# A gated recurrence with a channel MLP behind it: last chunk's second product and store in two parts, new orders and engines for most steps

## Chip, core and metric

The kernel runs on one core of one Trainium2 chip. The core has five engines that run their own instruction lists side by side: PE (TensorE: matmuls and weight loads), DVE (VectorE), ACT (ScalarE), POOL (GpSimd) and SP (SyncE, which here only issues DMAs). POOL issues DMAs too, on a queue of its own. The metric is the time of one execution on the device in microseconds (us).

## The reference

```
attention part, for each batch (4) and head (8), D = 48, t = 0 .. 767:
    mag = sqrt(a_re^2 + a_im^2);  a = (a_re, a_im) * min(mag, 0.999) / (mag + 1e-6)
    S = a * S (complex, a over the rows of S) + (k_t outer v_t, real)
    y_t = q_t @ S_re
x = y, heads side by side: 4 x 768 rows of 384
MLP part, for each row of x:
    xn = (x - mean) / sqrt(var + 1e-6) * g_ln
    out = x + max(xn @ w_ch1, 0) @ w_ch2         # w_ch1 384 x 1536, w_ch2 1536 x 384
```

## The kernel before

The 4 x 768 rows are cut into 24 chunks of 128 rows, six for each batch. Consecutive chunks form nine groups (0 holds chunk 0, 1 holds chunks 1 and 2, 2 holds 3 to 5, and so on by threes; 8 holds 21 to 23), and the groups form six phases.

**Gate steps of a group.** From the loaded a: `rec` (ln and exp of a_re on ACT), `r` = ai times that (one step for each chunk, on DVE or POOL), `r2` = its square, `l1p` (ACT), `lm` (DVE, L425), `cap` (DVE, L432: min with a constant, in place). PE sums the logarithms along the rows with a triangular matrix (`l_ps`, L438), and ACT makes `ep` and `en` of it (`epn`, L443). Another table of ACT is then loaded (L370) and the arctan of r taken (L493). `carry` steps add whole chunks, PE sums the angle (`th_ps`, L530 to L534), ACT takes the sine, DVE shifts by a quarter turn (`w`, L547), ACT takes the cosine. `qk` (L582) multiplies q by ep and k by en, `stk` (L588) multiplies both by sine and by cosine.

**Attention of a chunk.** stk is transposed to `qkt`: for chunks 0 to 11 by PE (`heads`, L615) and a copy by ACT or DVE, for chunks 12 to 23 by a transposing DMA that SP issues (L628). PE makes the scores (`a_ps`, L640), DVE masks them (`at`, L644), PE makes `y_ps` (L666, L668), and the state goes on to the next chunk by `t_ps` (PE) and `s` (DVE, L716).

**MLP of a chunk.** `x` is copied from y_ps, its moments are taken (`bn` on DVE, L737, or sums on ACT, L732), POOL makes `rs` for three chunks (L742, L743), x is transposed to `xt` (PE and a copy, or a DMA by SP, L756), `up` is the first product (`h_ps`, L778, 36 matmuls of 128 columns in parts of 24 and 12), `relu` (ACT L784 or DVE L786) makes `ht`, `down` is the second product (`o_ps`, L799, 12 matmuls of 384 columns), `residual` (DVE, L803) scales and adds x, `store` (SP, L807) writes 192 KB.

**Weights.** w_ch1 comes in three loads of 512 columns (`w1r`, POOL's queue, 384 KB each in SBUF) and is folded with g_ln: `centring` makes a matrix from g_ln (`gln`, one small load), PE multiplies it with w1r (`means`, `w_ps`, L318), DVE makes `w1c` (L322, three steps for each load). w_ch2 comes as three loads (`w2b`). The inputs of batch 0 are loaded chunk by chunk (a by SP, q and k by POOL), those of later batches six chunks at a time by POOL.

**What sets the order.** Every step is recorded in a plan with its engine, a cost, what it needs and what it makes. The kernel then issues all steps in one list, `HOW["order"]`, which holds their numbers; each engine runs its own steps in that order and waits where one is not ready. Where a step can run on several engines, a string in `HOW` has one letter for each step (A, V, P for ACT, DVE, POOL). `HOW["fill"]` names steps of PE ahead of which identity matmuls run that fill the step's own PSUM tile and are overwritten (L169 for bf16 tiles, L173 for others: 512 columns each in a wide tile). Some of DVE's and POOL's steps, cap among them, carry a flag `port` in the plan.

Of the kernel before, what the change touches and what calls it, by code (L numbers as in the profile page):

```python
# [10 lines left out]
FP32 = mybir.dt.float32  # L11
# [3 lines left out]
ALU = mybir.AluOpType  # L15
# [5 lines left out]

LOADS = {"a": ("ar", "ai"), "s": ("q", "k", "v"), "qk": ("q", "k"), "v": ("v",)}
HOW = {'loads': [('a', 0, 1, 'Y'), ('a', 1, 2, 'Y'), ('a', 2, 3, 'Y'), ('a', 3, 4, 'Y'), ('a', 4, 5, 'Y'), ('a', 5, 6, 'Y'),
           ('g', 0, 0, 'P'), ('w1', 0, 0, 'P'), ('w1', 1, 0, 'P'), ('w1', 2, 0, 'P'), ('qk', 0, 1, 'P'),
           ('qk', 1, 2, 'P'), ('qk', 2, 3, 'P'), ('qk', 3, 4, 'P'), ('qk', 4, 5, 'P'), ('qk', 5, 6, 'P'),
# [5 lines left out]
 'ar2': 'PPPPPPPPPPPPPPPPPPPPPPPP',  # L33
 'ai2': 'PPPPPPPPPPPPPPPPPPPPPPPP',
 'm2': 'PPPPPPPPPPPPPPPPPPPPPPPP',
 'r2': 'PVAVVAAAAVVVVVVVVVVVVVVV',
 'r': 'VVVVVVVVVPVVVPPPPPPPPPPP',
 'carry': 'VVVVPVVVVVPVVVVVPVVPVVVV',
 'st': 'AVVVVVAA',
 'x': 'AAAVAAAVAAVAAAAVAAAAAAAA',  # L40
 'edge': 'YYYYYYYYYYYYYYYYYYYYYYYY',
 'cos': 'VVVVVVVVVVVVVVVVVVVVVVVV',
 'qt': 'AAAAAVVVAVVVAAAAAAAAAAAA',
 'kt': 'AVVVAAVAVVVVVVVVVVVVVVVV',
 'relu': 'AAAVVVAAAAAVAVAAAVAAVAAAAAAAAVVVAAAAAAAAAAVAAAAA',
 'qk': 'PPVVVVPVPPVPVVVVVVVVVVVVVVVVVVVVVVVVVVVVVVVVVVVV',
 'stk': 'PVVVVVVVVVVVVVVVVVVVVVVVVVVVVVVVVVVVVVVVVVVVVVVV',
 'at': 'VVVVVVVVVVVVVVVVVVVVVVVV',
 'xc': 'AVAAAVAAVAVVVVVVVVVVVVVV',
 'xt': 'PPPPPPPPPPPPDDDDDDDDDDDD',  # L50
 'qkt': 'PPPPPPPPPPPPDDDDDDDDDDDD',
 'order': [5, 20, 38, 199, 8, 4, 12, 36, 40, 14, 16, 22, 18, 200, 201, 24, 202, 9, 203, 11, 28, 212, 44, 213, 46, 204,
           215, 48, 214, 42, 216, 186, 217, 1, 205, 191, 0, 206, 50, 218, 207, 54, 219, 208, 6, 193, 220, 209, 210,
           52, 221, 32, 2, 222, 34, 75, 7, 10, 225, 232, 231, 235, 226, 227, 236, 192, 238, 228, 26, 243, 229, 233,
           187, 239, 230, 240, 30, 68, 234, 241, 188, 470, 223, 246, 472, 190, 194, 66, 247, 242, 195, 237, 189, 248,
           197, 478, 60, 479, 471, 249, 62, 250, 473, 251, 56, 245, 252, 3, 244, 79, 253, 198, 64, 493, 516, 196, 494,
           495, 254, 81, 518, 517, 255, 496, 256, 480, 257, 474, 481, 258, 475, 259, 501, 503, 261, 519, 58, 497, 260,
           502, 476, 504, 264, 262, 520, 498, 265, 278, 499, 524, 500, 266, 521, 267, 268, 477, 505, 77, 483, 269,
           506, 484, 272, 88, 482, 522, 525, 487, 523, 271, 270, 528, 507, 485, 273, 529, 275, 274, 279, 526, 510,
           276, 486, 508, 95, 280, 277, 530, 282, 281, 532, 488, 511, 540, 283, 538, 541, 489, 531, 102, 284, 533,  # L60
           509, 563, 285, 539, 527, 512, 286, 287, 564, 288, 542, 109, 289, 513, 584, 490, 546, 561, 290, 534, 562,
           585, 547, 291, 543, 292, 548, 294, 582, 535, 295, 293, 544, 549, 545, 297, 569, 565, 296, 583, 551, 300,
           298, 310, 566, 586, 491, 514, 587, 301, 567, 568, 116, 302, 306, 570, 303, 307, 550, 552, 588, 308, 304,
           572, 311, 555, 123, 589, 305, 553, 573, 556, 312, 309, 592, 610, 574, 554, 313, 314, 611, 571, 602, 604,
           593, 315, 612, 603, 625, 605, 646, 316, 626, 606, 627, 607, 647, 317, 557, 628, 130, 319, 318, 575, 320,
           608, 629, 613, 576, 321, 630, 594, 577, 322, 137, 609, 648, 595, 615, 596, 323, 616, 327, 597, 324, 329,
           578, 590, 328, 325, 649, 591, 326, 614, 330, 633, 332, 343, 536, 558, 650, 617, 651, 333, 579, 631, 618,
           634, 334, 335, 580, 559, 632, 652, 342, 635, 336, 338, 654, 337, 339, 636, 619, 653, 340, 637, 655, 172,
           638, 341, 620, 344, 346, 598, 144, 345, 347, 658, 348, 670, 659, 599, 668, 671, 691, 600, 364, 350, 676,
           669, 693, 677, 714, 639, 692, 351, 640, 715, 365, 712, 349, 672, 694, 641, 660, 368, 673, 352, 366, 713,  # L70
           695, 353, 674, 696, 367, 621, 675, 158, 369, 354, 678, 370, 355, 681, 679, 356, 656, 642, 661, 371, 657,
           358, 357, 716, 372, 151, 682, 373, 717, 662, 374, 697, 663, 375, 376, 698, 699, 378, 359, 622, 664, 361,
           701, 377, 392, 360, 643, 381, 680, 644, 702, 362, 683, 703, 665, 623, 382, 404, 666, 704, 379, 684, 383,
           700, 391, 395, 384, 705, 718, 396, 385, 387, 719, 386, 388, 722, 685, 389, 706, 393, 390, 397, 707, 394,
           400, 398, 401, 723, 732, 740, 399, 686, 738, 726, 739, 402, 687, 741, 403, 753, 405, 406, 408, 724, 772,
           407, 409, 798, 759, 734, 410, 799, 760, 708, 735, 792, 727, 412, 725, 720, 736, 755, 721, 737, 728, 426,
           756, 743, 411, 427, 709, 813, 688, 774, 413, 757, 775, 778, 430, 758, 414, 762, 779, 776, 428, 729, 794,
           777, 747, 832, 415, 795, 429, 745, 165, 431, 416, 782, 800, 746, 796, 801, 815, 689, 797, 432, 764, 710,
           179, 816, 803, 819, 417, 765, 817, 433, 418, 748, 834, 419, 766, 835, 786, 420, 434, 421, 818, 784, 423,
           821, 822, 422, 761, 767, 435, 730, 785, 749, 780, 424, 454, 437, 802, 436, 438, 742, 768, 440, 439, 781,  # L80
           467, 443, 787, 805, 466, 444, 750, 824, 806, 457, 445, 769, 446, 825, 820, 770, 458, 449, 447, 453, 836,
           826, 450, 448, 837, 788, 840, 451, 455, 452, 751, 462, 456, 459, 463, 807, 789, 460, 850, 464, 844, 808,
           858, 845, 461, 842, 790, 827, 871, 838, 465, 856, 809, 468, 839, 843, 857, 890, 859, 469, 852, 828, 853,
           441, 854, 910, 829, 877, 855, 873, 846, 874, 861, 810, 878, 892, 931, 875, 893, 916, 896, 876, 897, 880,
           894, 912, 895, 918, 913, 811, 860, 863, 900, 898, 917, 919, 914, 830, 864, 847, 950, 865, 933, 915, 882,
           934, 920, 848, 879, 921, 902, 866, 899, 867, 903, 904, 935, 905, 884, 883, 937, 952, 885, 938, 923, 936,
           953, 940, 868, 925, 924, 954, 869, 926, 886, 955, 939, 958, 906, 887, 888, 944, 907, 960, 908, 945, 962,
           942, 927, 943, 956, 963, 957, 946, 961, 964, 947, 928, 929, 948, 965, 966],
 'fill': {227: 2.67, 256: 0.26, 470: 0.81, 493: 2.49}}


class Plan:
# [32 lines left out]
def kernel(  # L125
# [14 lines left out]
    C = 128  # L140
    NCH = S // C
    NG = B * NCH
    DM = H * D
    DF = moe_w_ch1.shape[1]
    NJ = DF // C
# [11 lines left out]
    moe = pool("moe", 2)  # L157
    V, A, P, T, Y = nc.vector, nc.scalar, nc.gpsimd, nc.tensor, nc.sync
    BY = {"V": V, "A": A, "P": P, "Y": Y}
    ENG = {V: "V", A: "A", P: "P", T: "T", Y: "Y"}  # L160

    fill = [0.0]
# [27 lines left out]
    def op(eng, us, needs, makes, fn, *a, **kw):  # L190
        if eng is T:
            kw["lag"] = 0.14
        return plan.add(ENG[eng], us, (fn, a), needs, makes, **kw)
# [31 lines left out]

    def load(eng, g0, g1, names, after=()):
        b, c0, c1 = g0 // NCH, g0 % NCH, g0 % NCH + g1 - g0
        us = 0.5 if eng is Y else 0.66 + 0.26 * (c1 - c0)
        for n in names:
            issue(eng, us, [("in_" + n, b)], load_fn, (eng, b, n, c0, c1), c1 - c0,  # L230
                  1.0, [("got_" + n, b, c) for c in range(c0, c1)])

    def over_sp(us, moves, lag, needs, makes, fn, *a, **kw):
        key = ("sp",) + makes[0]
        used = list(kw.pop("uses", ()))
        plan.add("Y", us, (fn, a), needs, makes + [key], uses=used, **kw)
        plan.add("Q", moves, None, [key], makes, uses=list(needs) + used, lag=lag, ring="Y")
# [58 lines left out]
    w2b = consts.tile([C, NJ, DM], BF16, name="w2b")  # L296
# [306 lines left out]
    stats = {}  # L603
# [123 lines left out]
    def feed(g):  # L727
# [65 lines left out]
            opt("relu", 2 * g + (j0 > 0), dict(A=0.17 + 0.107 * m, V=0.16 + 0.132 * m), [("h_ps", g, j0)], [("ht", g)],  # L793
                relu, j0, j1)

        def down():
            ps = ch["o_ps"] = narrow("o_ps", [C, DM])
            for i in range(NJ):
                T.matmul(ps, lhsT=ch["ht"][:, i], rhs=w2b[:, i], start=(i == 0), stop=(i == NJ - 1))  # L799

        def residual():
            ch["o"] = moe.tile([C, DM], FP32, tag="o", name="o", bufs=3)
            V.scalar_tensor_tensor(out=ch["o"], in0=ch["o_ps"], scalar=stats[u, "rs"][:, ds(j, 1)],  # L803
                                   in1=ch["x"], op0=ALU.mult, op1=ALU.add)

        def store():
            Y.dma_start(out=out[g // NCH, ts(g % NCH, C)], in_=ch["o"])  # L807

        op(T, 1.97, [("ht", g)] + [("W2", n) for n in range(3)], [("o_ps", g)], down, takes="nar")
        op(V, 0.61, [("o_ps", g), ("rs", u), ("x", g)], [("o", g)], residual)  # L810
        over_sp(0.35, 0.9, 1.5, [("o", g)], [("out", g)], store)


    w1v = moe_w_ch1.rearrange("(i p) j -> p i j", p=C)
# [6 lines left out]
    for what, g0, g1, eng in HOW["loads"]:  # L821
        if what not in LOADS:
            load_w(P, *weights[what, g0])
        else:
            load({"Y": Y, "P": P}[eng], g0, g1, LOADS[what])
    op(V, 0.5, [("gln",), ("c_ones",)], [("centre",)], centring, port=True)
    for n in range(DF // 512):
        fold(n)
# [43 lines left out]
```

## Time and profile before

| | us |
|---|---|
| median of 3 runs (lowest, highest) | 208.03 (207.81, 209.25) |
| profiled execution, its own time | 209.94 |
| span of that execution | 208.1 |
| PE busy | 172.7 (83%) |
| DVE busy | 158.3 (76%) |
| ACT busy | 150.6 (72%) |
| POOL busy | 95.0 (46%) |
| 36 x 24 matmuls h_ps, L778 | 54.4 |
| 12 x 24 matmuls o_ps, L799 | 50.2 |
| residual, L803, 24 steps of 0.611 | 14.4 |

The profile shows one execution, with times from the start of its span. Busy time leaves out waits and the issuing of DMAs. PE's matmuls are pipelined, so a matmul's own duration is longer than the distance to the next one: 48 matmuls of h_ps follow each other within 2.68 us. A row names line, engine, operation and tiles; "idle before <-" says what ended the engine's wait. SPq and POOLq are the queues that issue DMAs.

### The profile page before, as it was taken

How to read it: one execution, taken by the hardware profiler on the slowest of the kernel's cores; microseconds unless marked ns; L12 is line 12 of the kernel's file. 1: busy time of each engine (PE TensorE's matmuls, PEld its weight loads, DVE VectorE, ACT ScalarE, POOL GpSimd, SP SyncE). 2: the span in 40 equal slices, each digit the busy share in tenths (PEclk: the TensorE clock that was granted, in tenths of full speed). 3: DMA queues.
4: the chain of work that ended last, by engine and by line, in shares of the span. 5: the costliest groups of instructions: out<-in, count | busy, mean ns of one | idle time of the engine just before them, and what ended most of it. 6: DMA issues, size and time to landing. Idle time of an engine off the chain costs nothing.

```text
span 208.1 us, 5401 instructions
## 1 busy us (share of the span) xinstructions
PE 172.7 (83%) x2287; PEld 134.8 (65%) x2287; DVE 158.3 (76%) x258; ACT 150.6 (72%) x211; POOL 95.0 (46%) x87
## 2 busy tenths in 40 slices
PE   0008969789879899999989989997999896999992
PEld 0003449669657788777956767696777665988861
DVE  0156599999879999799999999899699974606202
ACT  2247697998959999989997969896996614456150
POOL 5099698265092916699879300992210400020020
PEclk9999975999999999999999999999999998899999
DMA  6999999999999999997998919799992999723303
GB/s 101 206 180 154 200 87 148 225 115 219 166 78 143 137 238 197 123 184 71 160 161 175 265 54 269 157 215 176 161 88 71 164 206 201 194 78 55 99 3 113
DMA packets 124932, 31.44 MB, mean 151 GB/s; under 512 B 117420, under 2 KB 123276, under 8 KB 124908
## 3 DMA queue, kind: packets, MB, share of 16 engines
q0 software_dynamic: 78720, 16.52, 90.4%
q1 hardware_dynamic: 46188, 14.57, 32.0%
q8 instruction: 18, 0.29, 0.6%
q14 instruction: 6, 0.05, 0.1%
HBM read 28.31 MB, written 4.72 MB: 159 GB/s over the span
## 4 chain that ended last, share of the span: by engine, by line
PE 37%; DVE 17%; issue 13%; POOL 11%; DMA 10%; ACT 6%; SPq 4%; POOLq 0%; ACTq 0%; DVEq 0%
PE o_ps L799 12%; PE h_ps L778 11%; DMA ar<-in_a_re_dram 4%; POOL qk L213 4%; DVE stk L588 3%; DMA xt<-x 3%; DMA qkt<-stk 3%; DVE w L547 3%; PE qk_ps L169 2%; DVE at L644 2%; POOL ai L213 2%; SPq L628 2%; PE a_ps L640 2%; PE qk_ps L615 2%; PE th_ps L173 2%
## 5 line engine op out<-in xcount | busy, mean ns | idle before, releaser
L778 PE MATMUL h_ps<-xt,w1c 128*128 128x128 bf16 x864 | 54.4, 221 | 1.6 <-DMA xt<-x 1.3
L778 PEld LDWEIGHTS <-w1c 128*128 128x128 bf16 x864 | 50.5, 99 | 3.1 <-DMA xt<-x 1.5
L799 PE MATMUL o_ps<-w2b,ht 128*128 128x384 bf16 x288 | 50.2, 326 | 0.2 <-ACT ht L784 0.2
L784 ACT ACTIVATE ht<-h_ps 128x1024 bf16<-128x1024 f32 (+1 forms) x37 | 29.7, 821 | 14.9 <-PE h_ps L778 14.9
L799 PEld LDWEIGHTS <-ht 128*128 128x128 bf16 x288 | 27.4, 98 | 17.0 <-ACT ht L784 0.3
L644 DVE TENSOR_TENSOR at<-a_ps,mask 128x1024 bf16<-128x1024 f32 x24 | 29.2, 1220 | 6.4 <-PE a_ps L640 5.9
L742 POOL TENSOR_SCALAR rs<-mv 128x3 f32<-128x3 f32 x8 | 3.6, 450 | 52.0 <-ACT junk L732 33.4
L803 DVE SCALAR_TENSOR_TENSOR o<-o_ps,rs,x 128x384 f32<-128x384 f32 x24 | 14.4, 611 | 14.3 <-PE o_ps L799 10.3
L443 ACT ACTIVATE epn<-l_ps 128x384 bf16<-128x384 f32 (+1 forms) x32 | 18.7, 652 | 5.3 <-PE l_ps L438 5.3
L391 POOL TENSOR_TENSOR r<-ai,m 128x384 bf16<-128x384 f32 x12 | 11.7, 999 | 16.5 <-ACT m L412 16.5
L640 PE MATMUL a_ps<-qkt 128*128 128x128 bf16 x192 | 15.1, 223 | 2.5 <-DMA qkt<-stk 2.2
L318 PE MATMUL w_ps<-w1r,centre 128*128 128x512 bf16 x9 | 3.6, 527 | 16.2 <-DVE centre L308 15.4
L615 PE MATMUL qk_ps<-ident,stk 128*128 128x128 bf16 x192 | 13.2, 220 | 3.8 <-DVE stk L588 2.2
L370 ACT ACT_TABLE_LOAD x12 | 15.4, 1283 | 0.9 <-PEq L856 0.7
L409 ACT ACTIVATE rec<-ar 128x1152 f32<-128x1152 f32 (+2 forms) x9 | 9.5, 1055 | 8.8 <-DMA ar<-in_a_re_dram 8.7
L716 DVE TENSOR_TENSOR s<-t_ps,dec 128x384 bf16<-128x384 f32 x20 | 11.0, 551 | 6.2 <-PE t_ps L711 5.9
L391 DVE TENSOR_TENSOR r<-ai,m 128x384 bf16<-128x384 f32 x12 | 6.3, 562 | 11.4 <-DMA ai<-in_a_im_dram 9.0
L640 PEld LDWEIGHTS <-qkt 128*128 128x128 bf16 x192 | 11.7, 99 | 4.0 <-DMA qkt<-stk 2.7
L615 PEld LDWEIGHTS <-stk 128*128 128x128 bf16 x192 | 11.3, 98 | 4.6 <-DVE stk L588 1.7
L666 PE MATMUL y_ps<-v,at 128*128 128x48 bf16 x192 | 12.4, 184 | 2.2 <-DVE at L644 2.2
L582 POOL TENSOR_TENSOR epn<-qk,epn 128x1152 bf16<-128x1152 bf16 (+1 forms) x6 | 11.2, 1879 | 4.2 <-ACT epn L443 4.2
L666 PEld LDWEIGHTS <-at 128*128 128x128 bf16 x192 | 10.8, 96 | 3.5 <-DVE at L644 2.7
(102 smaller groups left out, 371.4 us busy)
## 6 DMA issues: line engine op xcount, KB each, us to landing
out_dram<-o SPq DMA_DIRECT2D x24, 192.0 KB, 3.9
ar<-in_a_re_dram POOLq DMA_DIRECT2D x3, 1152.0 KB, 10.5
ai<-in_a_im_dram POOLq DMA_DIRECT2D x3, 1152.0 KB, 11.5
v<-in_v_dram POOLq DMA_DIRECT2D x4, 576.0 KB, 10.7
qk<-in_q_dram POOLq DMA_DIRECT2D x3, 576.0 KB, 12.6
qk<-in_k_dram POOLq DMA_DIRECT2D x3, 576.0 KB, 9.5
ar<-in_a_re_dram SPq DMA_DIRECT2D x6, 192.0 KB, 5.5
w1r<-in_moe_w_ch_dram POOLq DMA_DIRECT2D x3, 384.0 KB, 6.7
```

Source lines behind the costliest of these rows:

```text
L213: eng.dma_start(out=inp[n, b].rearrange("p h c d -> p (h c) d"), in_=view.rearrange("p h c d -> p (h c) d"))
L370: op(A, 1.28, old, [key], lambda: A.preload_act_table_set(TABLES[which]))
L391: times = lambda eng, out, x, y: eng.tensor_tensor(out=out, in0=x, in1=y, op=ALU.mult)
L443: A.activation(out=o, in_=banks(G["l_ps", j], m), func=AF.Exp, scale=(1.0, -1.0)[s])
L615: T.transpose(ps[:, h], G["stk"][:, int(which == "ks"), j, ts(h, C)], K["ident"])
L640: T.matmul(ch["a"][:, h], lhsT=ch["kt"][:, h], rhs=ch["qt"][:, h], start=True, stop=True)
L644: V.tensor_tensor(out=ch["at"], in0=ch["a"], in1=K["mask"].unsqueeze(1).to_broadcast([C, H, C]), op=ALU.mult)
L666: T.matmul(hd(ps)[:, h], lhsT=ch["at"][:, h], rhs=vt[:, h, c], start=True, stop=sp is None)
L778: T.matmul(ps[:, jj], lhsT=w1c[:, i, ts(j0 + jj, C)], rhs=ch["xt"][:, i], start=(i == 0), stop=(i == ND - 1))
L784: A.activation(out=o, in_=i, func=AF.Relu)
L799: T.matmul(ps, lhsT=ch["ht"][:, i], rhs=w2b[:, i], start=(i == 0), stop=(i == NJ - 1))
L803: V.scalar_tensor_tensor(out=ch["o"], in0=ch["o_ps"], scalar=stats[u, "rs"][:, ds(j, 1)], in1=ch["x"], op0=ALU.mult, op1=ALU.add)
```

## The change

The last chunk's second product, residual and store are made in two parts of 192 columns: two PSUM tiles with 12 matmuls each, two residuals, two stores of 96 KB. The plan has four steps more for it. a can now be loaded as ar and ai apart, and by ACT's queue too, though the list of loads is as it was. Engine strings, order and fills are new.

```diff
-        def down():
-            ps = ch["o_ps"] = narrow("o_ps", [C, DM])
-            for i in range(NJ):
-                T.matmul(ps, lhsT=ch["ht"][:, i], rhs=w2b[:, i], start=(i == 0), stop=(i == NJ - 1))
...
+        parts = 2 if g == NG - 1 else 1
+        w = DM // parts
+        def down(i):
+            ps = ch["o_ps", i] = narrow("o_ps", [C, w])
+            for jj in range(NJ):
+                T.matmul(ps, lhsT=ch["ht"][:, jj], rhs=w2b[:, jj, ds(i * w, w)], start=(jj == 0), stop=(jj == NJ - 1))
+        def residual(i):
...
+            at = ds(i * w, w)
+            V.scalar_tensor_tensor(out=ch["o"][:, at], in0=ch["o_ps", i], scalar=stats[u, "rs"][:, ds(j, 1)],
+                                   in1=ch["x"][:, at], op0=ALU.mult, op1=ALU.add)
+        def store(i):
+            at = ds(i * w, w)
+            Y.dma_start(out=out[g // NCH, ts(g % NCH, C), at], in_=ch["o"][:, at])
...
- 'fill': {227: 2.67, 256: 0.26, 470: 0.81, 493: 2.49}}
+ 'fill': {207: 7.0, 227: 0.55, 259: 1.05, 470: 1.14, 472: 1.67, 495: 1.24}}
```

Step 207 is the first l_ps (32 filling matmuls), 227 the first th_ps (12 before, 2 after), 470 and 472 the transposes of chunk 0, 495 and 493 those of chunk 1, 256 and 259 the l_ps of group 2.

Steps by engine that differ in number, over the whole kernel:

```
                       before              after
relu                   37 ACT, 11 DVE      33 ACT, 15 DVE
xt copies (chunks <12)  7 ACT,  5 DVE       3 ACT,  9 DVE
qkt copies             10 ACT, 14 DVE       9 ACT, 15 DVE
qk                     12 DVE,  6 POOL     10 DVE,  8 POOL
stk                    17 DVE,  1 POOL     16 DVE,  2 POOL
carry                   6 DVE,  4 POOL      5 DVE,  5 POOL
```

The first part of three lists, from the order of instructions (numbers behind q, k, ar, ai are chunks, behind w1r thirds):

```
SP before    ar2 ar0 ai0 ar1 ai2 ai1 ar3 ar4, edge of group 0, ar5 ai5 ai3 ai4
SP after     ar0 ar2 ar1 ai0 ai1 ai2 ar4 ar3, edge of group 0, ar5 ai5 ai4, edge of group 1, ai3
POOL before  w1r0, gln, w1r1, library reload, r2 of chunk 0, q0 k0 q1, w1r2, ident, u_half, k1 k2 q2,
             u_turn, w2b, qk qk and stk of group 0, v
POOL after   w1r1, ident (with the library reload), gln, r of chunk 0, w1r0, w1r2, q2 k1, u_half, q0 k5,
             u_turn, k0 k2 q1, w2b, mask, qk of group 0, carry carry, stk of group 0, v
DVE after    constants, r r, padding, lm of group 0, centring, lm of group 1, cap cap, u_back, base,
             seven w1c, padding, qk of group 0, w w, qk and stk of groups 0 and 1, w1c w1c, r r r, r2,
             qt of chunk 0, lm and cap of group 2
```

ident is the identity that PE's filling matmuls and transposes need. SP's list from the first transposing DMA of batch 3:

```
before   qkt18, out, qkt19, qkt20, edge, qkt21, xt18, qkt22, xt19, out, xt20, out, qkt23, out, xt21 ...
after    qkt18, qkt19, out, qkt20, qkt21, xt18, qkt22, xt19, xt20, out, out, qkt23, xt21, out, out ...
         (the edge of group 8 stands ahead of qkt18)
```

POOL's list behind the exps of group 7 is rs, carry, rs before, and qk qk (group 7), rs, carry, carry, qk, stk (the sine half of group 8), rs after; the steps added there were DVE's.

## The prediction

> **What bounds the kernel now.** I read the busy time of each engine in stretches of 10 us first (columns: busy us and instruction count of PE, weight loads, DVE, ACT, POOL, then the granted clock of TensorE, the DMA share and GB/s), because the kernel passes through stages with different limits.
>
> ```profile
> 0.00:10.00 10.00, 0.00 (x0) 0.00 (x0) 0.95 (x9) 2.33 (x3) 2.68 (x7) 1.00 0.92 150
> ...
> 30.00:40.00 10.00, 8.38 (x100) 7.76 (x100) 9.68 (x15) 8.19 (x10) 6.81 (x8) 0.73 2.21 175
> ...
> 120.00:130.00 10.00, 9.31 (x117) 7.01 (x115) 9.97 (x15) 8.17 (x11) 0.07 (x1) 1.00 0.69 155
> ...
> 170.00:180.00 10.00, 7.99 (x126) 6.90 (x124) 5.91 (x9) 3.06 (x9) 0.00 (x0) 0.83 0.82 171
> 180.00:190.00 10.00, 10.00 (x169) 9.06 (x167) 3.43 (x5) 6.28 (x14) 1.05 (x2) 1.00 0.38 92
> ```
>
> Four stages. Up to 15 us nothing but loads and short gate steps; from 25 to 160 us DVE, PE and ACT are all nearly full (DVE 9.97 of 10 at 120, PE 9.31); at 165 to 180 everything has gaps; from 180 PE alone is full to the end. Then the chain of waits, in order of time (start, us, what), for who sets the pace in the thin stages:
>
> ```profile
> 2.74 8.96 DMA ar<-in_a_re_dram
> 11.79 0.85 ACT rec L409
> 12.66 0.85 ACT m L412
> 13.54 1.04 DVE r L391 x2
> ...
> 17.34 0.37 DVE lm L432
> 17.75 0.80 PE l_ps L438 x2
> ...
> 169.05 0.78 SPq L447
> ...
> 169.96 5.55 DMA qkt<-stk
> 175.55 1.03 PE a_ps L640 x8
> ...
> 204.48 0.62 DVE o L803
> ```
>
> At the start a load of ar sets the pace, at 165 to 176 SyncE's queue and a transposing DMA, at the end the last residual. Last, DMA traffic in stretches of 2 us, here 4 to 6 us (packets, MB, share of 16 engines):
>
> ```profile
> q0 software_dynamic: 265, 0.27, 98.6%
> q1 hardware_dynamic: 155, 0.03, 10.3%
> ```
>
> While POOL's two w1r loads run, SyncE's a loads nearly stop.
>
> **The change part by part.** Order and engine choice change for most steps, so I price by stage.
>
> *Start, to cap of group 2 (DVE L432 at 36.45 us, done at 37.2).* Before, two w1r loads (384 KB each on the page) are issued at 1.23 and 2.97 us; the six a loads of phase 0 need 1.18 MB and SyncE's queue had moved 1.16 MB only at 12 us. After, only one w1r is issued early; the other two stand behind POOL's r of chunk 0. That is 0.38 MB less in front of the sixth a load; at the 196 to 217 GB/s of the stretches 6:8 and 8:10 it is 1.8 to 1.9 us. SyncE also sends all three ar before the ai, so the two ACT steps at 11.79 and 12.66 (0.85 each) leave the path, while r2 goes from DVE (0.56) to ACT (0.84 by the 768-column rows): another -1.7 + 0.3. So l_ps of group 1 comes 1.9 to 3.3 us before 17.75. Behind it DVE works through its list without a pause: seven w1c of 0.66, then padding 0.70, qk 0.35, w 0.44 and 0.86, qk and stk of groups 0 and 1 (three of 0.5, two of 0.95), two w1c, three r of 0.50, r2 0.70, qt 0.62, lm 1.35 and cap 0.45: 16.5 us. It can begin when the first late w1r is there: r of chunk 0 done about 9.5, issue 0.76, landing 5.5 to 8.0 (the three w1r rows), so 16 to 18 us; 17.5 + 16.5 gives cap at 34 against 37.2. Ends: 0 (a landing that eats all of it) and -3.1; I take **-2.0**, nearer to the bandwidth row than to the full chain. The 32 filling matmuls now ahead of l_ps (before, 12 ahead of th_ps took 4.44 us, 0.43 each at the pace of a cold array) need 12 x 0.43 and 20 x 0.217 (the o_ps rate, 1.95 for 12 of 384 columns), 9.5 us from about 3.5; they end at 13, a little before l_ps is ready at 14.5 to 16, and that wait covers them. All at the cold pace they would end at 17, and each us later costs one.
>
> *Middle, cap of group 2 to cap of group 8 (144.7).* By the two orders DVE gets four xt copies (0.35), one bn (0.73), two carries (0.36), one r (0.50) and a dec (0.17) more, one relu (0.69) and one x (0.55) less: +2.3. ACT's total hardly moves. Against that, three of the seven caps of 1152 columns took 0.75, 0.88 and 0.95 where the other four took 0.46, and each of the three lay beside a POOL DMA issue (those of 36.94, 104.35 and 139.45); planned clear of those, two of them in this stage give back 0.9. Net +1.4 at most on an engine with 6 us of idle in 105. Ends 0 and +2.3; I take **+1.0**.
>
> *165 to 176 us.* SyncE's list from the first qkt of batch 3 was qkt, out, qkt, qkt, edge (0.78), qkt, and PE waits 1.69 us at 175.55 for that fourth qkt. The new list has the edge ahead of all four: 0.78 and its 0.1 around less, and a pause of 0.46 before the second qkt with it: -1.3 at the fourth issue. DVE also loses three qk (0.75), a stack (1.35) and a carry before it, 3.9 us in all, so stk of group 7 is not later. They go to POOL, which lies nearly empty there: its list becomes qk, qk, rs, carry, carry, qk, then stk for the sine of group 8, of 2304 columns. POOL's row for 768 columns is 1.88, so this is up to 5.6. POOL's qk can start at 146.8 (after the exps) and takes 2 x 2.36 + 1.1 + 1.8 + 2.36 = 10, done by 157.5 since the carries wait for the arctan at 153; the sine of group 8 ends at 161.2, so stk is done by 166.8 against 166.7 on DVE, 3 us before its transpose is issued at 169.96. Hidden; beyond 170 every us is one us. I take **-1.3**; ends +1 and -2.9, the latter with the clock: after that gap the 24 h_ps matmuls took 2.14 us where 36 take 2.01 at 188.20, some 1.6 lost with a_ps and t_ps. A pause of 1.69 us was enough for a granted clock of 0.66 in 175 to 180. The Trainium skill (TensorE: Matmul & The Clock Gate, Part 1) has the clock fall only after an idle window of about 3.4 us; by that no shorter gap would matter and the 1.6 would stay. The trace disagrees here, as no gap at 165 to 180 is that long.
>
> *Tail.* The last 12 o_ps matmuls of 384 columns become 24 of 192: same columns, weights loaded twice, but loads run at 56 ns beside h_ps and a 192-column matmul needs 81. So PE is even. After the last one, DVE's 0.62 becomes some 0.36 to 0.41 (half the columns of a row whose fixed part is about 0.15), and the last store moves 96 KB: a 192 KB store ran at 380 GB/s, 0.5 us, so 0.25 less. Ends -0.1 and -0.6; **-0.4**.
>
> Sum: -2.0 + 1.0 - 1.3 - 0.4 = -2.7. The profiled execution took 209.94 us (span 208.1 and 1.8 around it), so 207.2; it was 0.9% above the median of the runs, and by ratio the forecast is 208.03 x 207.2 / 209.94 = **205.3**.
>
> **Rivals.** (1) *The start gains nothing.* In the new POOL list a library reload (an ISA instruction) and the making of ident stand ahead of the gln load. Before, that reload lay in POOL's idle 6.44 us before 10.16. If it takes all of that, gln is issued at 9.5, lands at 15.8 (6.3 on the page), and centring, which DVE holds ahead of lm, puts l_ps of group 1 at 18. Then -0.7: 207.3. Against it: no packet on an instruction queue before 30 us. The Trainium skill (GPSIMD Engine Reference, 2.1 Instruction dispatch) puts the first call after such a load at about 6 us with no visible instruction; this trace only bounds it by 6.4. (2) *Slower: the weights come too late.* DVE's seven w1c now stand ahead of all of group 0. POOL's two w1r and six qk loads follow each other from 9.5 on, beside SyncE's other six a loads: 0.77 + 0.59 + 1.18 MB, at 150 to 200 GB/s done between 22 and 26. If the w1r share evenly, DVE starts its list not at 17.5 but at 23, cap at 39.5 to 40: +3.0 in place of -2.0, so +2.3: 210.3. It decides where the first w1c starts later than 20.7; for it, the starved queue above; against it, SyncE's share was already moved earlier. (3) *All gains in full*, start -3.1 and the clock kept: -5.4 to -4.3: 202.7 to 203.8.
>
> **How the numbers follow.** Forecast 0.37, (1) 0.26, (2) 0.24, (3) 0.13. A measurement of this kernel can tell some 1%, 2.1 us, from no change. Faster than 205.95: three quarters of the forecast (0.28), all of (3), 0.02 of (1): 0.43. Within 1%: the rest of the forecast and of (1), 0.33. Slower than 210.1: (2), 0.24. Range 202.7 to 210.4: from the best of (3) to just past (2)'s 210.3, so about half of (2) lies outside; the forecast's own is 204 to 206.6.
>
> **What would show it.** Start: the first l_ps of group 1 near 15 us, the first w1c near 17.5, cap of group 2 near 35; rival (1) shows gln's centring at 16, rival (2) DVE idle before w1c or qk until 21 and later. Middle: caps of 1152 columns all at 0.46, and the time from cap 2 to cap 8 (107.5 now) longer by 1. Late stage: a_ps of chunk 21 less than 1 us idle before it, granted clock above 0.66 after it, POOL's stk done before its qkt is issued. Tail: under 3.3 us from the last o_ps matmul to the end, 3.7 now. The forecast is wrong if the middle stretches by over 3 us, which no row prices, since nearly every list is reordered there.

## The result, and the profile after

| | before | after |
|---|---|---|
| median (lowest, highest), us | 208.06 (207.81, 209.25) | 215.11 (213.82, 217.76) |
| ratio, 95% interval | | 1.031 [1.024, 1.037] |
| profiled execution, span | 209.94, 208.1 | 215.37, 213.6 |
| mean granted clock, profiled execution | 0.975 | 0.960 |

The change makes the kernel 7 us slower. The prediction, 205.3 in a range up to 210.4, was wrong. The ratios here and below leave disturbed runs out and so can differ a little from a quotient of medians.

Busy time in stretches of 10 us, after (columns as before: PE, weight loads, DVE, ACT, POOL, granted clock, DMA share, GB/s):

```profile
0.00:10.00 10.00, 7.16 (x26) 2.93 (x27) 0.40 (x7) 3.11 (x4) 2.41 (x8) 1.00 0.79 140
30.00:40.00 10.00, 7.60 (x82) 6.86 (x81) 8.39 (x12) 5.84 (x7) 7.09 (x8) 0.66 1.99 142
120.00:130.00 10.00, 9.20 (x121) 6.97 (x121) 9.54 (x14) 8.94 (x13) 2.16 (x2) 1.00 1.52 144
140.00:150.00 10.00, 4.56 (x88) 4.22 (x87) 4.20 (x6) 4.89 (x5) 1.09 (x1) 0.98 2.11 127
170.00:180.00 10.00, 8.80 (x94) 6.02 (x91) 7.37 (x11) 2.66 (x4) 4.98 (x3) 1.00 1.17 185
180.00:190.00 10.00, 9.02 (x192) 8.58 (x191) 6.37 (x9) 5.75 (x16) 1.05 (x2) 1.00 0.84 200
```

Of the stretches that the prediction looked at, 30 to 40 is thinner than before (PE 7.60 for 8.38, DVE 8.39 for 9.68), 120 to 130 about the same, 170 to 180 fuller. A new hole has opened at 140 to 150: PE 4.56 of 10, DVE 4.20, ACT 4.89. All three stood still there together. Before, the same stretch read:

```profile
140.00:150.00 10.00, 8.57 (x123) 6.93 (x121) 8.58 (x16) 8.03 (x13) 2.74 (x3) 1.00 2.10 162
```

The chain of waits after, in order of time, says for what:

```profile
1.85 7.28 DMA ar<-in_a_re_dram
...
9.22 0.85 ACT rec L409
10.07 0.98 POOL r L391
...
19.11 10.07 DMA qk<-in_q_dram
...
132.37 5.13 DMA qkt<-stk
...
139.97 9.39 DMA qkt<-stk
...
149.41 0.93 PE a_ps L640 x8
...
173.50 6.30 DMA qkt<-stk
...
210.19 0.42 DVE o L810
```

The ar that sets the pace at the start lands at 9.13 in place of 11.70, but a load of q for chunk 1, issued at 19.11, then takes 10 us. Three transposing DMAs stand in the chain; the one of chunk 17 takes 9.39 us from issue to landing (before, the same one was issued at 136.97 and its a_ps began 5.4 later). DMA traffic at 4 to 6 us is as before, so the early loads of a still give way to POOL's queue:

```profile
q0 software_dynamic: 297, 0.30, 101.3%
q1 hardware_dynamic: 134, 0.02, 7.0%
```

DVE's timeline around the hole (start, us, line, operation, idle before it):

```profile
143.15 0.45 DVE L432 TENSOR_SCALAR lm<-lm 128x1152 bf16<-128x1152 bf16 x1
143.52 0.68 DVE L786 TENSOR_SCALAR ht<-h_ps 128x512 bf16<-128x512 f32 x1
150.38 1.23 DVE L644 TENSOR_TENSOR at<-a_ps,mask 128x1024 bf16<-128x1024 f32 x1 [6.18 <-PE a_ps L640]
151.52 1.35 DVE L425 SCALAR_TENSOR_TENSOR lm<-rec,m 128x1152 bf16<-128x1152 f32 x1
152.90 0.46 DVE L432 TENSOR_SCALAR lm<-lm 128x1152 bf16<-128x1152 bf16 x1
```

The mask of chunk 17 waits for its a_ps, and lm and cap of group 8 stand behind that mask (before, lm stood ahead). Cap to cap (cap 2 stands for the cap of group 2): cap 2 starts at 37.99 (before 36.45), cap 6 at 110.44 (109.30), cap 8 at 152.90 (144.27). From cap 6 to a_ps of chunk 17 it takes 39.0 us, 33.0 before; from there to the end 64.2, 65.7 before. Most of the loss sits between cap 6 and that a_ps.

### The profile page after: what moved, and what is told of

Same layout as the page of the kernel before. It is cut to its first block, busy times and chain, and to the rows that moved or that the text cites. A ratio compares the mean times of both kernels' runs of the same rounds, so it can differ in the third digit from the quotient of the medians.

```text
span 213.6 us, 5529 instructions
## 1 busy us (share of the span) xinstructions
PE 180.9 (85%) x2337; PEld 139.0 (65%) x2337; DVE 160.2 (75%) x264; ACT 144.2 (68%) x202; POOL 108.1 (51%) x91
## 4 chain that ended last, share of the span: by engine, by line
PE 37%; DMA 18%; DVE 14%; POOL 13%; issue 10%; ACT 5%; SPq 0%; POOLq 0%; ACTq 0%; DVEq 0%
PE h_ps L778 13%; PE o_ps L804 13%; DMA qkt<-stk 10%; DMA qk<-in_q_dram 5%; DMA ar<-in_a_re_dram 3%; POOL qk L213 3%; DVE at L644 3%; POOL qk L215 2%; PE qk_ps L615 2%; DVE stk L588 2%; DVE w L547 2%; PE a_ps L640 2%; POOL r L391 2%; ACT epn L443 2%; PE qk_ps L169 2%
## 5 line engine op out<-in xcount | busy, mean ns | idle before, releaser
L804 PE MATMUL o_ps<-w2b,ht 128*128 128x384 bf16 (+1 forms) x300 | 50.6, 319 | 0.4
L804 PEld LDWEIGHTS <-ht 128*128 128x128 bf16 x300 | 28.2, 98 | 16.4 <-issue 0.6
L644 DVE TENSOR_TENSOR at<-a_ps,mask 128x1024 bf16<-128x1024 f32 x24 | 29.2, 1220 | 10.8 <-PE a_ps L640 10.5
L784 ACT ACTIVATE ht<-h_ps 128x1024 bf16<-128x1024 f32 (+1 forms) x33 | 26.5, 813 | 15.2 <-PE h_ps L778 11.0
L582 POOL TENSOR_TENSOR epn<-qk,epn 128x1152 bf16<-128x1152 bf16 (+1 forms) x8 | 17.4, 2182 | 21.2 <-ACT epn L443 20.1
L786 DVE TENSOR_SCALAR ht<-h_ps 128x512 bf16<-128x512 f32 (+1 forms) x15 | 14.0, 933 | 9.8 <-PE h_ps L778 7.6
L810 DVE SCALAR_TENSOR_TENSOR o<-o_ps,rs,x 128x384 f32<-128x384 f32 (+1 forms) x25 | 14.6, 594 | 6.9 <-PE o_ps L804 5.2
L615 PE MATMUL qk_ps<-ident,stk 128*128 128x128 bf16 x192 | 14.3, 227 | 4.2 <-DVE stk L588 4.2
L391 POOL TENSOR_TENSOR r<-ai,m 128x384 bf16<-128x384 f32 x12 | 11.8, 1005 | 10.5 <-ACT rec L409 6.5
L615 PEld LDWEIGHTS <-stk 128*128 128x128 bf16 x192 | 12.2, 102 | 5.5 <-POOL stk L588 3.6
L422 ACT ACTIVATE m<-lm,one 128x1152 f32<-128x1152 bf16 (+2 forms) x9 | 10.3, 1148 | 5.4 <-DVE lm L391 5.2
L213 POOL DMA_DIRECT2D qk<-in_k_dram x3 | 6.7, 2241 | 13.8 <-issue 7.0
## 6 DMA issues: line engine op xcount, KB each, us to landing
ar<-in_a_re_dram POOLq DMA_DIRECT2D x3, 1152.0 KB, 10.9
```

Of the source, the lines that this page charges most:

```text
L391: times = lambda eng, out, x, y: eng.tensor_tensor(out=out, in0=x, in1=y, op=ALU.mult)
L582: eng.tensor_tensor(out=o, in0=part(G, "qk"[s]).rearrange("p h c d -> p c h d"), in1=i, op=ALU.mult)
L615: T.transpose(ps[:, h], G["stk"][:, int(which == "ks"), j, ts(h, C)], K["ident"])
L644: V.tensor_tensor(out=ch["at"], in0=ch["a"], in1=K["mask"].unsqueeze(1).to_broadcast([C, H, C]), op=ALU.mult)
L784: A.activation(out=o, in_=i, func=AF.Relu)
L786: V.tensor_scalar(out=o, in0=i, scalar1=0.0, scalar2=None, op0=ALU.max)
```

## The experiments

Eighteen kernels. The table sorts them by a property that I did not know of until the sixteenth had run: where in SBUF the two tiles lie from which the transposing DMAs read, `stk1` (chunks 12 to 14 and 18 to 20) and `stk0` (15 to 17 and 21 to 23). The numbers in brackets say how far the address lies above a multiple of 256 bytes. The addresses are those of the built programs. No trace holds them, but the distances between them follow from the sizes of the constants and the order in which each kernel makes them.

| stk1, stk0 | kernels: median us |
|---|---|
| 36864 (0), 50432 (0) | before 207 to 208, tail_only 208.0, late_only 207.8, after_from_110 206.5; with loads of POOL moved: q_early 212.4, collide 217.1 |
| 36832 (224), 50688 (0) | after 215.1, need_order 214.4, w1r_early 216.3, q_late 213.7, lm_first 213.2, r_first 211.9, v_late 211.8, combined2 211.2, edge_first 210.3, combined 210.1, start_only 214.9, after_to_110 214.9 |
| 36864 (0), 50752 (64) | aligned 211.4 |
| 36864 (0), 50944 (0) | aligned_all 207.5 |

### First theory: a load collides with the transposing DMA

POOL's load of v for batch 3 was issued at 138.78, the transposing DMA of chunk 17 at 139.97. While it hangs, from 146 to 148, the software queue has nearly all of the traffic (packets, MB, share of 16 engines):

```profile
q0 software_dynamic: 2099, 0.20, 497.5%
q1 hardware_dynamic: 79, 0.02, 8.6%
```

Theory C: this meeting is the loss. Theory L: the new lists make everything late there, and the transfer with it.

**v late.**

```diff
 POOL: r r r (group 8)
-      load v (batch 3)   k x en (group 7)
+      k x en (group 7)   load v (batch 3)
```

> The changed kernel with one instruction moved: POOL's load of v for batch 3 stands behind its first qk of group 7 and so is issued some 8 us later. Theory C (collision): the transposing DMA of chunk 17 took 9.4 us because that load's packets filled the DMA engines; without it, it takes some 4.4, cap of group 8 starts near 147 to 148 in place of 152.9, and the time falls by 4 to 6 us to 209 to 211. Theory L (the lists): the stretch from 140 to 150 us is thin because engine choices and SyncE's order make everything late there, the transfer is only late with the rest; then the time stays at 214 to 216. If the load is then too late for the y_ps of chunk 18 (about 170 to 173 us), a wait shows there and part of the gain is lost.

211.8 us (1.024 [1.016, 1.033]). a_ps of chunk 17 came 5.4 us behind the issue, not 9.4, and cap 8 5.4 behind cap 7, not 9.8. So the meeting is worth some 4 us in the trace, but only 3.3 came back in the median, and by the ratio 0.7%, 1.4 us, with intervals that overlap. C explains half at most.

**r first, and q and k in the order of need.**

```diff
 POOL: load q (batch 2)
-      load k (batch 2)   r (chunk 11)
+      r (chunk 11)   load k (batch 2)
```

> The changed kernel with POOL's r of chunk 11 (group 4) ahead of the load of k for batch 2, which is blocked until PE has freed its buffer. DVE's wait of 2.0 us before lm of group 4 should go, cap of group 4 start near 84 in place of 85.98. If such delays are carried to the end: 213, 2 less. If the later stages absorb them (theory C, where the transfer of 140 to 149 us sets the end by itself): 214.5 to 215.5.

```diff
-POOL: q2 k1 u_half q0 k5 u_turn k0 k2 q1 w2b
+POOL: q0 k0 u_half q1 k1 u_turn q2 k2 w2b k5
```

> The changed kernel with POOL's first loads of q and k in the order of need (q0 k0 q1 k1 q2 k2, then a part of w2b, then k5). The load of q for chunk 1, issued at 19.11 and landed at 29.2 in the changed kernel, should land near 26, DVE's wait of 1.59 us at 26.1 go, and cap of group 2 start near 36.5 in place of 38.0. Carried to the end: 213.5. If the queue is served in such a way that all six land together (bandwidth), nothing changes at 29 and the time stays at 215.

r first: 211.9 (1.024 [1.017, 1.030]); DVE's wait is gone, cap 4 at 83.20 in place of 85.98, and from cap 2 to cap 6 it takes 71.5 us in place of 72.5. The median fell by 3.2. Of the 3.1 us between the two profiles, 1.0 lies there and 1.2 ahead of cap 2, which the move does not touch. Order of need: 214.4 (1.032 [1.022, 1.042]). Cap 2 came at 36.24, but kernels with the untouched start had it at 36.6 and 36.8 as well; the 37.99 of the first profile was partly chance. The move itself gained nothing that can be seen.

**The tail alone.**

```diff
 (the kernel before, its lists)
-down, residual, store of chunk 23
+down 1, ..., down 0, residual 1, residual 0, store 1, store 0
```

> The kernel before with only the split of the last chunk's second product, residual and store. All theories: everything up to 204 us as before, and 0.3 to 0.4 us less at the end, so 207.7 of 208.06. If the second tile, its weight loads or the second store cost more than they hide: 208.3 to 209.

208.0 against 207.3 (1.000 [0.996, 1.005]). Nothing that can be measured. Its profile is useful as a second look at the kernel before: a_ps of chunk 17 33.0 behind cap 6 and 63.2 to the end.

**lm first, edge first, and all together.**

```diff
-DVE: at (chunk 17)   lm, cap (group 8)
+DVE: lm, cap (group 8)   at (chunk 17)
```

> The changed kernel with DVE's lm and cap of group 8 ahead of the mask of chunk 17 (as they stand, lm ahead, in the kernel before). The load of v stays where it collides. Theory C with the order (the transfer of chunk 17 is late, and DVE's lm of group 8 waits behind the mask that needs it): cap of group 8 starts near 145 in place of 152.9, PE still idles some 3.8 us before a_ps of chunk 17, and the time falls by 2 to 4 to 211 to 213. If only the transfer counts: PE is the pace, 214 to 216. If the order is the whole cause: 209 to 210.

```diff
-SP: qkt12 qkt13   edge 6   qkt14 qkt15
+SP: edge 6   qkt12 qkt13 qkt14 qkt15
```

> The changed kernel with SyncE's edge of group 6 ahead of all the transposing DMAs, as before. The one of chunk 17 is issued near 139.1 in place of 139.97. Theory C: 0.9 us less of it lies beside the load's packets, so it lands 0.9 to 2 us sooner and the time is 213 to 214.5. Theory L (SyncE's order is the cause): 211 or less. If nothing hangs on it: 215.

> The changed kernel with all four moves: v of batch 3 late, r of chunk 11 ahead of the load of k, lm and cap of group 8 ahead of the mask of chunk 17, edge of group 6 first. Late v alone took 3.3 us off, r first 3.2 (in single medians that scatter by some 1.5). If they add, with 1 to 2 from the other two: 206 to 208, at or below the kernel before (207.3). If late v and lm first mend the same delay: 208 to 209.5.

lm first: 213.2 (1.025 [1.018, 1.033]); cap 8 at 145.1, but PE still waits for chunk 17, so little is gained. Edge first: 210.3 (1.010 [1.004, 1.017]), far more than its 0.9 us: a_ps of chunk 17 came 6.9 behind the issue. What the meeting costs is no simple function of the load's lead: at 1.0 us it is 6.9 here, at 1.2 it was 9.4 in the changed kernel and 7.8 in lm first. Combined: 210.1 (1.012 [1.006, 1.019]), no better than edge first alone. Four fixes whose medians lie 2 to 5 us lower each do not add, and 2 to 3 us remain.

**The meeting made in the kernel before.**

```diff
 (the kernel before)
 POOL: carry (group 6)
+      load q (batch 3)
       r (four of groups 7 and 8)
+      load v (batch 3)
       r r (group 8)
-      load q (batch 3)   load v (batch 3)
```

> The kernel before with two of POOL's loads moved: q of batch 3 as early as in the changed kernel (near 119 us), and v of batch 3 ahead of the last two r of group 8, so that it is issued some 1.8 us ahead of the transposing DMA of chunk 17 in place of 2.5 behind it. Theory C: that DMA takes 8 to 10 us from issue to a_ps in place of 5.4, cap of group 8 starts near 148 in place of 144.3, and the time rises by 3 to 4, to 210.5 to 212. Without a collision only the 2.3 us by which the two r come later are left: cap of group 8 near 145.5 and 208 to 209.

217.1 (1.039 [1.030, 1.048]), more than expected, because q hit too. Its packets ran from 123 to 129, and until 128 the first transposing DMA, issued at 124.79, hardly moved. DMA traffic from 126 to 128 in this kernel:

```profile
q0 software_dynamic: 2512, 0.24, 230.7%
q1 hardware_dynamic: 15, 0.00, 0.8%
```

The meeting is real and dear. That did not make it the cause: in this kernel, as in every one with the new lists, the first four transposing DMAs of batch 2 took 10.5 to 10.9 us to issue (an edge of 0.8 among them in most), in place of 7.9. So I suspected the early load of q in both.

**q late, and q early in the kernel before.**

```diff
 (the changed kernel)
-POOL: q x ep (group 6)   load q (batch 3)   ...   load v (batch 3)
+POOL: q x ep (group 6)   ...   load q (batch 3)   load v (batch 3)
```

> The changed kernel with POOL's load of q for batch 3 back where it stood before, ahead of the load of v and behind the r of group 8, so that q is issued near 138 us in place of 116 and v 2.3 us later. Theory C2 (both loads of batch 3 get in the way of SyncE's transposing DMAs: four of them were issued in 10.5 us in place of 7.9 wherever q came early, and v then held up the one of chunk 17): the four are issued in 8 us, chunk 17's a_ps comes 5.4 us after its issue, cap of group 8 near 146, time 208 to 210. Theory L (the pace of the four has nothing to do with q): still 10.5 us; the v load comes 2.3 later, which alone gives 212 to 213.

> The mirror image: the kernel before with only the load of q for batch 3 early, near 119 us; v then takes its place at 137.2. C2: the four transposing DMAs are issued in 10.5 us in place of 7.9, the one of chunk 17 then meets v's packets; cap of group 8 at 147 to 149, time 210 to 213. If early q does nothing by itself: 208.

> The changed kernel with q of batch 3 late, r of chunk 11 ahead of the load of k, lm and cap of group 8 ahead of the mask of chunk 17, and the edge of group 6 first. C2: the stretch to cap of group 8 as short as before, the late stage and the tail of the change kept: 206 to 208, about the kernel before or 0.5 less. If the late stage gives nothing either: 208 to 209.

q late: 213.7 (1.032 [1.025, 1.039]); 4.68 and 5.13 us for the two pairs, as slow as in the changed kernel (4.69 and 5.25). q early: 212.4 (1.023 [1.017, 1.030]), 10.7 for the four. Two different things look alike in SyncE's list: a load that stops them (q early, collide), and a slow pace with no load near. Combined2: 211.2 (1.017 [1.010, 1.024]). C2 falls; the slow pace had no cause yet.

**One more w1r early.**

```diff
 POOL: gln
+      w1r0
       r (chunk 0)
-      w1r0
       w1r2
```

> The changed kernel with one more load of w1r early, right behind gln (3.5 us) in place of 11.0. The prediction's start: the early l_ps and the early w1c exclude each other, because both hang on the same DMA traffic. The sixth a load 1.8 us later, l_ps of group 1 near 17 in place of 15.3, the first w1c near 17.5 in place of 19.0, cap of group 2 near 36, within 1 us of the changed kernel; time 214 to 215.5. If the traffic does not matter: l_ps stays at 15.3, w1c at 17, cap of group 2 near 34.5, time 213.

216.3 (1.042 [1.035, 1.049]). l_ps of group 1 at 17.06 in place of 15.26: one load of w1r ahead costs 1.8, as the prediction had it. The first w1c came at 19.5, no sooner, since PE makes w_ps behind l_ps. Cap 2 at 36.57.

### Second theory: which stretch makes the loss

Four hybrids: one kernel's list, engines and fills up to a point, and behind it what is left of the other's list in its own order.

```diff
-list: before
+start_only:     after up to cap 2, then before
+after_to_110:   after up to cap 6, then before
+after_from_110: before up to cap 6, then after (split tail included)
+late_only:      before up to cap 8, then after (split tail included)
```

> The changed kernel's list and engines up to the cap of group 2, and everything behind it as in the kernel before. The prediction's -2.0: cap of group 2 near 34.5, time 205.5. What the runs so far suggest (cap at 35.1 to 38.0 with the new start, 36.5 to 37.8 with the old): some 1 us, time 206.5 to 207.5. If the lists don't fit together behind it: 208 or more.

> The changed kernel's list and engines up to the cap of group 6 (some 110 us), and the kernel before's behind it. If the whole loss is made behind 110: the four transposing DMAs of batch 2 in 7.9 us, a_ps of chunk 17 33 us behind cap 6, time 206 to 209 (the wait of DVE for POOL's r near 82 stays in it). If the slow pace of the four is made before 110: 10.5 us, and 209 to 211.

> The mirror image: the kernel before up to the cap of group 6, the changed kernel behind it. If the whole loss is made behind 110: the four in 10.5 us, the one of chunk 17 in 8 to 9.5, a_ps of chunk 17 38 to 39 us behind cap 6, time 213 to 215. If half of it is made before: 209 to 211.

> The kernel before up to the cap of group 8, the changed kernel behind it, split tail included. The prediction's -1.3 and -0.4: the fourth transposing DMA of batch 3 1.3 us sooner, a_ps of chunk 21 with less than 1 us idle before it, time 205.8 to 206. If the late stage only follows a_ps of chunk 17 (64 us from it to the end in all kernels so far, within 1.5): 207.3, the tail alone.

start_only 214.9 (1.045 [1.036, 1.054]), after_to_110 214.9 (1.038 [1.028, 1.048]), after_from_110 206.5 (1.000 [0.995, 1.005]), late_only 207.8 (1.004 [0.998, 1.010]). As the origin of the loss both theories fall: everything behind 110 us of the changed kernel costs nothing on the old start, and the new start alone costs all of it, although its cap 2 comes at 36.37, no later than before. The loss is made in the first 37 us and shows 90 us later. SyncE's list of start_only, whose steps there are those of the kernel before (7.90 for the four):

```profile
124.18 10.38 SPq L623 DMA_TRANSPOSE qkt<-stk  x4
```

and of the kernel before:

```profile
123.35 7.90 SPq L628 DMA_TRANSPOSE qkt<-stk  x4
```

What the start leaves behind is memory. Constants are placed in SBUF in the order in which they are made; the new order puts 32 bytes less ahead of stk1, at 36832 in place of 36864.

### Third theory: the address

**Aligned.** Two unused tiles of 32 bytes; no instruction changes.

```diff
-        K["stk", i] = consts.tile([C, GMAX * 2 * H * 2, DP], BF16, name=f"stk{i}")
+        consts.tile([C, 8], FP32, name=f"gap{i}"); K["stk", i] = consts.tile([C, GMAX * 2 * H * 2, DP], BF16, name=f"stk{i}")
```

> The changed kernel with two unused tiles of 32 bytes, one ahead of each stk tile, so that stk1 lies at 36864 and stk0 at 50752, both multiples of 64; no instruction changes. Theory M (the address of what a transposing DMA reads): two of them in a row are issued in 3.9 us in place of 4.7, a_ps of chunk 17 comes 33 to 34 us behind cap 6 in place of 39, no wait of 3.8 us before it, and the time is 206 to 208, level with the kernel before or up to 2 below. Theory S (something else in the new start, the clock or a queue): 213 to 216, the pace of the transposing DMAs as in the changed kernel.

211.4 (1.020 [1.014, 1.026]): a third to a half of the loss is gone. The trace says why. DMA traffic of the changed kernel (queue, packets, MB, share; transposing DMAs issued, median us to landing) at 126 to 128, when they read stk1 (36832):

```profile
q1 hardware_dynamic: 1667, 0.43, 114.9%
...
qkt<-stk SPq DMA_TRANSPOSE x2, 4.8
```

and at 138 to 140, when they read stk0 (50688):

```profile
q1 hardware_dynamic: 2094, 0.53, 116.8%
...
qkt<-stk SPq DMA_TRANSPOSE x2, 3.7
```

In aligned, at 124 to 126 from stk1 (now 36864):

```profile
q1 hardware_dynamic: 2267, 0.57, 126.4%
```

and at 135 to 137 from stk0 (now 50752), with an xt transpose among them:

```profile
q1 hardware_dynamic: 1658, 0.42, 113.3%
```

The kernel before, from stk1 at 36864, at 126 to 128:

```profile
q1 hardware_dynamic: 2106, 0.53, 125.6%
```

Counted record by record, the busiest whole microsecond has 1135 packets of 256 bytes from stk1 (chunks 12 to 14) and 835 from stk0 (chunk 16) in aligned; in the changed kernel it is the other way round, 845 (chunks 12 and 13) and 1127 (chunks 15 and 16). My gaps had mended stk1 and shifted stk0 and all that lies behind it by 64 bytes: the slow pace went over to stk0. Within each kernel a DMA of the same size, on the same queue, is slow from the one tile and fast from the other. The tile moves; the pace goes with it, with one exception. In aligned the DMA of chunk 15, from stk0 64 above the boundary, begins at about 165 packets in 0.2 us, nearly stands still from 131.2 to 132.2, and its rest then goes at about 226 in 0.2 us, the fast pace. Chunk 14 does the same after a standstill in the changed kernel, start_only and q_late. So the slow pace is seen only from addresses off the boundary, but not all the time there; why it ends after a standstill stays open. I had taken a multiple of 64 for enough; it is not.

**All aligned.** Gaps of 32 and 224 bytes; stk1, stk0 and x all at their old distance from a multiple of 256.

```diff
-        consts.tile([C, 8], FP32, name=f"gap{i}"); ...
+        consts.tile([C, (56, 8)[i]], FP32, name=f"gap{i}"); ...
```

> The changed kernel with gaps of 32 bytes ahead of stk1 and 224 ahead of stk0: stk1 at 36864, stk0 at 50944, both multiples of 256, x as before at 128 above one; no instruction changes. Theory M: every transposing DMA of qkt at the pace of before (two in a row in 3.9 us), a_ps of chunk 17 33 to 34 us behind cap 6, a_ps of chunk 23 some 40 us behind that, and 205.5 to 207.5: the change without its side effect, to be held against the prediction's 205.3. If v's load still meets the transposing DMA of chunk 17 although that is issued 2 us sooner: 208 to 210. If the address is not it: 211 or more.

207.45, 12 runs (204.89 to 210.81), against 207.69, 17 runs (206.27 to 210.39): 0.997 [0.992, 1.001]. The hole in busy time is closed:

```profile
140.00:150.00 10.00, 8.98 (x129) 6.98 (x127) 7.85 (x14) 7.44 (x13) 4.28 (x2) 1.00 1.44 141
```

One part of the expectation was missed: the first pair of transposing DMAs is issued in 3.85 us, but the second, of chunks 14 and 15, still in 4.69, although both tiles lie at a multiple of 256. The hardware queue moved only 62 packets from 130 to 131 there. A packet of 16 KB on an instruction queue starts at 129.46, and in the ten profiles compared a standstill of about 1 us follows such a packet (before: packet at 132.89, standstill from 133.6 to 134.6, behind the four DMAs). No run takes that packet away, so the link is not shown.

With not one instruction changed, the ratio to the kernel before goes from 1.031 to 0.997. It does not beat the kernel before by more than the measurement can tell, nor does after_from_110, which has the lowest median. Not tried: r first on top of it, and the reverse, stk1 of the kernel before at 36832.

The chain of causes, then: stk1 lies 224 above a multiple of 256; transposing DMAs read from it at 0.8 of the pace (4.8 us to landing in place of 3.7 to 4.2), so the four of chunks 12 to 15, three of which read stk1, take 1.4 us longer to issue than in aligned_all with the same lists (9.94 in place of 8.54, the edge between them not counted; 7.90 in the kernel before); the one of chunk 17, itself fast, is issued 1.2 us behind the load of v, 0.2 ahead of it in aligned_all, and that load holds it up for 4 us; PE, DVE and ACT all wait, and after the 3.8 us pause of PE the granted clock is 0.70 from 150 to 155. This is why v late, edge first and lm first each gave back some us: they cut the chain at a later link. Where q is loaded late (start_only, after_to_110, q_late, combined2), it is the load of q that the DMA of chunk 17 meets. The 20 profiles agree with this link. Where a load of POOL is issued 1.0 us or more ahead of that DMA, a_ps comes 6.8 to 9.6 us behind its issue (11 profiles); where it comes behind the DMA, or there is none, 4.6 to 6.2 (7, the kernel before and aligned_all among them). Between, at 0.5 and 0.7 us, stand 5.2 (q_early) and 8.6 (aligned).

The Trainium skill (DMA: Bandwidth & Descriptors, How a descriptor splits into AXI transactions) states that a descriptor that does not start at a multiple of 256 bytes begins with a transaction from the boundary below it. A packet of these DMAs is 256 bytes in the trace, so each would need two transactions in place of one. The direction agrees: 1667 and 1658 packets against 2094 and 2267. By that page's counting, 15 beats in place of 8 at 224 above the boundary is an estimate of 1.9 times, and 10 in place of 8 at 64 above it one of 1.25 times. The trace has nearly the same pace at both, and it fell by 1.26 to 1.37; so the beats do not give the size, and why it is this size no run shows. The same page (DMA Transpose (X-bar), Constraints) asks for 32 bytes, which both addresses satisfy: that was enough to run here, not to run at full pace.

## Why the prediction was wrong, and where it was right

**The failed step: the middle.** "Ends 0 and +2.3; I take +1.0." Cap 2 to cap 8 took 114.9 us, 107.8 before: +7.1. Every term of that step counts instructions that were moved between engines and takes their durations from the rows of before. That is what failed: an unwritten assumption that a step which keeps its engine keeps its duration. The step said itself that the forecast is wrong "if the middle stretches by over 3 us, which no row prices, since nearly every list is reordered there". It looked for the danger in lists. It was in the addresses, which the order of the very first steps sets, and which can be read from the program before it runs. With the addresses mended the same stretch took 109.7 (aligned_all) and 109.0 (after_from_110): +1.9 and +1.2. So the terms that it did count were about right. All caps of 1152 took 0.45 to 0.46, as it said.

**Start, -2.0: right in kind, half in size.** l_ps of group 1 at 15.26, 2.5 sooner, within its 1.9 to 3.3. Cap 2, over the twelve profiles with the unchanged new start, lies at 35.1 to 38.0, mean 36.2; over six with the old start at 36.5 to 37.8, mean 37.2. That is -1.1. What is missing lies with the first w1c (17.5 to 19.0, 18.0 on average, not 17.5), with the chain behind it (18.0 us in aligned_all, where 16.5 was forecast without a pause; its rows as listed add up to 16.3) and, in the first profile, with the load of q for chunk 1.

**Rival 1 fell.** The library reload cost nothing that can be seen: ident's select ran at 2.49, gln was issued at 2.74, and PE's filling matmuls, begun at 2.84, were done, as the forecast had it, well before l_ps was ready: PE then waited 3.7 us.

**Rival 2: right that it is slower, for another reason.** A burst of loads does delay DVE (1.59 us at 26.1, for k), through q and k rather than w1r; cap 2 came at 36.2 on average, not at 39.5 to 40.

**165 to 176 us, -1.3: right, where the addresses allow it.** PE's wait before a_ps of chunk 21, 1.69 in the profile of before and 1.77 in tail_only, is gone in late_only and aligned_all; in the changed kernel PE waits 1.08 before the a_ps of chunk 20 instead, as chunks 18 to 20 read stk1. POOL's stack took 4.55, and SyncE's transpose of it came later: hidden. From a_ps 17 to a_ps 21 it takes 30.8 us in aligned_all, 32.3 in tail_only. In late_only, where only this and the tail are changed, the time does not show it (1.004 [0.998, 1.010]).

**Tail, -0.4: too small to be seen.** Last o_ps to the end 3.4 in place of 3.7; the time of tail_only is 1.000 [0.996, 1.005].

**The sum.** -2.7 was forecast; without the address the change takes -0.7, between -1.7 and +0.2 (0.997 of 207.7). By the terms as measured it would be -1.1 + 1.9 - 1.5 - 0.3 = -1.0. So the forecast without the missing term was 1.7 to 2 too low, by the start and the middle, and would have been within its range; the missing term was some 7 us.

A caution on all these sums: aligned_all's profile is of an execution of 204.89 us, 1.2% below its median, and before's of one 0.9% above. The profiles differ by 5.0 us, the medians by 0.2.

## What to carry to other kernels

A change of order is also a change of memory where tiles are placed as they are made: compare the addresses of what DMAs read, not only the lists, and keep the sources of transposing DMAs at multiples of 256 bytes (64 and 224 above one were slow here; for stk nothing else was tried). When several independent repairs each give back a part and together no more than one of them, look for a cause upstream of all. To find it, cut the change in time (first part of one list, rest of the other) before cutting it by theory: the four hybrids showed what the twelve kernels before them had not.

## What the runs showed of the hardware that I had not expected

- A transposing DMA's pace depends on the address of its source: 1667 and 1658 packets in 2 us at 224 and 64 above a multiple of 256, 2094 to 2267 at a multiple. In four profiles what was left after a standstill of the queue went at the fast pace from these addresses too.
- A load on the software queue nearly stops the hardware queue: 2512 packets against 15 in 2 us (collide). In the changed kernel a transposing DMA took 9.4 us beside one.
- A pause of PE can cost twice. Before the same 48 matmuls of h_ps PE waited 2.24 us in edge_first and 1.76 in v_late (start, us, idle before):

```profile
82.13 4.31 PE L778 MATMUL h_ps<-xt,w1c 128*128 128x128 bf16 x48 [2.24 <-DVE xt L752]
```

```profile
82.01 2.85 PE L778 MATMUL h_ps<-xt,w1c 128*128 128x128 bf16 x48 [1.76 <-DVE xt L752]
```

The first had a granted clock of 0.50 from 84 to 86 and took 1.5 us longer for these alone; the second kept 1.00. In edge_first, lm_first, q_late and w1r_early, all with this wait and a reduced clock there, cap 2 to cap 6 took 74.1 to 74.8 us, in v_late, need_order and aligned_all 72.1 to 72.5. It is not the length alone: the 1.69 us at 175 in the profile of before came with 0.66, the 1.77 at the same place in tail_only with 1.00. The Trainium skill (TensorE: Matmul & The Clock Gate, Part 1) puts the slow clock behind an idle window of about 3.4 us. The trace does not agree: the clock fell after 2.24. A part of the scatter between executions of one kernel may come from such pauses; that was not tried.
